# Three units in the first quarters, one SP ring for loads and transposes, layer norm of chunk 1 ahead of the first gates

## The chip, the core and the metric

The kernel runs on one core of a Trainium2 chip. The metric is device time in microseconds (us) of one execution; lower is better. Before the change the median of three runs is 571.9 us (571.53 to 572.21). The core has TensorE (PE in the profile, with its weight loads as PEld), VectorE (DVE), ScalarE (ACT), GpSimd (POOL) and SyncE (SP). Each takes its instructions in program order. SP, ACT and POOL also issue DMAs, each on a queue of its own, and 16 DMA engines move the data.

## What is computed

```python
x  = A_x                                   # 2048 x 448, bf16
xn = layernorm(x)
# A: sliding block of a cache: the last 512 of 2048 keys, 16 query heads of 256, 8 kv heads
q  = xn @ wq                               # 448 -> 4096
p  = softmax(q k^T / 16)                   # 2048 x 512 for each head
s  = concat(p v) @ wo                      # 4096 -> 448
# B: gated feed-forward of 1792 columns
g  = silu((gelu(xn @ w_gate) * (xn @ w_up)) @ w_down)
return x + s * g
```

## The kernel before

The 2048 rows are 16 tiles of 128 (`t`), four tiles make a chunk of 512 (`c`). All engines' instructions are recorded in one list; a small planner (`Plan`) derives the waits from readers and writers of each buffer and then emits each engine's instructions in the order in which they were recorded. So the order of the calls is the order on every engine and on every queue.

First comes the feed-forward part. A **unit** (`n`, 56 in all) is one block of 128 of the 1792 columns for one chunk: gate and up, each 448 deep. 448 is three times 128 and a rest of 64, and everything is cut into halves of 64 rows, so that a matmul on rows 0 to 63 and one on rows 64 to 127 run side by side. `group` writes a unit in two phases, of eight matmuls (with the rest rows, `wgur`) and of six; a unit takes two neighbouring PSUM banks, of the eight. Units go in groups of two; a group is 28 matmuls of 512 columns. `gu_evac` empties a unit: gelu on ACT from the gate's bank into `gl`, then a multiply on DVE of the up's bank and `gl` into `actT`. After a chunk's 14 units, `down` multiplies `actT` by `wd` (56 matmuls), and ACT and DVE make of it `g2`, which is the silu gate doubled.

Layer norm goes by tile: statistics on DVE (`ln_stats`), the inverse deviation either with ACT and DVE (tiles 0 to 3) or on POOL (`ln_rstd_pool`, the others), the normalized tile `xn` on DVE (`ln_norm`), and a transpose to `xnT`. Tiles 0 to 3 are transposed by PE (`ln_tp_pe`, into PSUM, with a copy by ACT or DVE), the others by a DMA transpose on SP (`ln_tp_dma`).

The **head** is the start: the first two units are computed in four quarters (`part`), of 128 columns each, as soon as each of tiles 0 to 3 is there. After each later unit's evacuation, `ln_step` does one step of the layer norm of the next tile: statistics, then, a unit later, norm and transpose.

Loads: x tiles 0 to 3 and the first weights on SP and ACT, further weights and x tiles 4 to 7 on SP, all at the start. Weights come in three blocks of columns whose bounds are in `FBL`. POOL loads x tiles 8 to 11, `wd` and x tiles 12 to 15 after units 4, 6 and 8; when the last tile is normalized, `wq`, V, `wo` and the first tiles of x for the residual (`xr`) on POOL, and K, with a DMA transpose, on SP.

Then comes attention: for each chunk, and each half of eight heads (`g`), four `q_group` of two heads make `qT`; for each head `s_mm` makes the scores and ACT their exponentials (`expT`), `pv` multiplies by V, DVE divides (`onorm`), and DMA transposes on SP make `oT`. `wo_mm` and `wo_fin` multiply by `wo`, gate, add x and store. The last chunk's `down` stands behind the first scores. In SBUF the attention tiles lie over the feed-forward ones; `K.reuse` adds the waits for that.

Of the kernel before, what the change touches and what calls it, by code (L numbers as in the profile page):

```python
# [5 lines left out]
ACT = mybir.ActivationFunctionType  # L6
# [5 lines left out]
P = 128  # L12
# [152 lines left out]
def bass_recurrent_scan__sliding_block_cached__geglu_ffn__prompt_kernel(  # L165
# [18 lines left out]
    NT = S // P  # L184
# [17 lines left out]
    with es:  # L202
# [50 lines left out]
        NXR = 4  # L253
# [21 lines left out]
        FBL = [0, 2, 6, NF]  # L275
# [6 lines left out]
        NGL = 4  # L282
        gl, a, at = place("gl", [P, NGL, QC], BF16, at=at)
        b_gl = sbuf_bufs(a, QC * 2, NGL)
        qT, a, at = place("qT", [P, HG, 2, QC], BF16, at=rf)
        b_qT = [[K.buf(a + (h * 2 + e) * QC * 2, QC * 2) for e in range(2)] for h in range(HG)]
        NEX = 3
        expT, a, at = place("expT", [P, NEX, NJ, QC], BF16, at=at)
# [4 lines left out]
        oT, a, at = place("oT", [P, NCO, QC], BF16, at=at)  # L293
        b_oT = [[K.buf(a, at - a) for t in range(4)] for p in range(Hq // 2)]

# [5 lines left out]
        out_view = out.rearrange("b (t p) d -> p (b t) d", p=P)  # L301

# [39 lines left out]
        load_wr("sp", 0, 1)  # L342
# [16 lines left out]
        load_w("sp", 2, 1)  # L359

# [57 lines left out]
        def group(units, x, lo, hi, start, stop, reads):  # L418

            for ph in range(2):
                for i, (b, w, wr) in enumerate(units):
                    lst = []
                    for k in ([NK] if ph == 0 else []) + list(range(NK)):
                        for u, j in ((0, ph), (1, 1 - ph)):
                            rows = slice(R * u, R * u + R)
                            l = wr[rows] if k == NK else w(j, k)[rows]
                            lst.append((bank[b + j][:, lo:hi], l, x(k)[rows], start and k == NK,  # L430
                                        stop and ph == 1 and k == NK - 1))
                    o = mms(lst, reads, b_ps[b:b + 2], [last_row[b]] if b in last_row else [])
                    last_row[b] = o

        def xs(c, lo=0, hi=QC):
            return lambda k: xnT[:, k, c * QC + lo:c * QC + hi]

        def gu_group(n, b, part=None):

            c, f0 = divmod(n, NF)  # L440
            units, deps = [], [b_wgu]
            for i in range(2):
                f = f0 + i
                wi = [j for j in range(3) if FBL[j] <= f][-1]
                deps += b_wl[wi] + b_wlr[min(wi, 1)]
                cols = slice(f * P, (f + 1) * P)
                units.append((b + 2 * i, lambda j, k, cols=cols: wgu[:, j, k, cols], wgur[:, cols]))
            lo, hi = (0, QC) if part is None else (part * P, (part + 1) * P)
            group(units, xs(c, lo, hi), lo, hi, lo == 0, hi == QC,
                  deps + b_xnT[c * 4 + lo // P:c * 4 + hi // P])  # L450
# [8 lines left out]
        def down(c, b0):  # L459
            for t4 in range(4):  # L460
                t = c * 4 + t4
                b = b0 + t4
                mms([(bank[b][:, 0:D], actT[:, c % 2, f, t4 * P:(t4 + 1) * P], wd[:, f, :], f == 0, f == NF - 1)
                     for f in range(NF)], [b_wd] + b_actT[c % 2], (b_ps[b],))
                s = t % 2
                act(tmp[:, s, :], bank[b][:, 0:D], ACT.Tanh, (b_ps[b],), b_tmp[s], scale=0.5)
                K.op("dve", lambda e, t=t, b=b, s=s: e.scalar_tensor_tensor(  # L467
                    out=g2[:, t, :], in0=tmp[:, s, :], scalar=1.0, in1=bank[b][:, 0:D],
                    op0=ALU.add, op1=ALU.mult), b_tmp[s] + [b_ps[b]], (b_g2[t],))

        def ln_first(t):
            ln_stats(t)
            ln_std_act(t)
# [10 lines left out]
        ln_tp_pe(0, 4, "act")  # L484
        ln_stats(2)
        ln_std_act(2)
        ln_tp_pe(1, 5, "dve")
        gu_group(0, 0, 0)
        gu_group(0, 0, 1)
        ln_second(2)  # L490
        ln_first(3)
        ln_tp_pe(2, 6, "act")
        gu_group(0, 0, 2)
        ln_second(3)
        ln_tp_pe(3, 7, "dve")

        act(tmp[:, 1, 0:1], nhalf[:, :], ACT.Gelu_apprx_tanh, (b_nhalf,), (b_tmp[1][0],))
        gu_group(0, 0, 3)
# [15 lines left out]
        DOWN_AT = {NF + 2: 0, 2 * NF + 2: 1, 3 * NF + 2: 2}  # L514
        cur = 0
        ln_t = [4, 4]

        def ln_step():

            t = ln_t[0]  # L520
            if t < NT and t == ln_t[1]:
                ln_stats(t)
                ln_rstd_pool(t)
                ln_t[0] += 1
            elif ln_t[1] < NT:
                t = ln_t[1]
                ln_norm(t)
                ln_tp_dma(t)
                ln_t[1] += 1

        for n in range(0, NQC * NF, 2):
            if n > 0:
                gu_group(n, cur)
            gu_evac(n, cur)
            if n > 0:
                ln_step()
            gu_evac(n + 1, cur + 2)
            if n > 0:
                ln_step()
            cur = 4 - cur  # L540
            if n == 4:
                load_x("pool", 8, 4)
            if n == 6:
                dma("pool", wd[:, :, :], B_w_down.rearrange("(f p) d -> p f d", p=P), (), (b_wd,))
            if n == 8:
                load_x("pool", 12, 4)
            if ln_t[1] == NT:
                ln_t[1] += 1
                for g in range(NG):
                    load_wq(g)  # L550
                for g in range(Hkv):
                    load_v(g)
                for g in range(Hkv):
                    load_k(g)
                K.reuse(b_wo)
                for i in range(NCO // 8):
                    dma("pool", wo[:, i * 8:(i + 1) * 8, :],
                        A_wo.rearrange("(c p) d -> p c d", p=P)[:, i * 8:(i + 1) * 8, :], (), (b_wo[i],))
                for t in range(NXR):
                    dma("pool", xr[:, t, :], x_view[:, t, :], (), (b_xr[t],))  # L560
            if n + 2 in DOWN_AT:
                down(DOWN_AT[n + 2], cur)
                cur = 4 - cur

        act(tmp[:, 1, 0:1], nhalf[:, :], ACT.Exp, (b_nhalf,), (b_tmp[1][0],))


        def q_group(c, h, b):

            units = [(b + 2 * i, lambda j, k, i=i: wq[:, k, (h + i) * Dh + j * P:(h + i) * Dh + (j + 1) * P],  # L570
                      wqr[:, h + i, :]) for i in range(2)]
            group(units, xs(c), 0, QC, True, True, b_wql[h // HG] + b_xnT[c * 4:c * 4 + 4])
            for i in range(2):
                h8, bb = h % HG + i, b + 2 * i
                act(qT[:, h8, 0, :], bank[bb], ACT.Copy, (b_ps[bb],), (b_qT[h8][0],))
                K.op("dve", lambda v, h8=h8, bb=bb: v.tensor_copy(qT[:, h8, 1, :], bank[bb + 1]),  # L576
                     (b_ps[bb + 1],), (b_qT[h8][1],))

        def s_mm(h, b0):
            h8, g = h % HG, h // 2  # L580
            x = h % NEX
            for jp in range(NJ // 2):
                for j in (2 * jp, 2 * jp + 1):
                    mms([(bank[b0 + j], kT[:, g, e, j * P:(j + 1) * P], qT[:, h8, e, :], e == 0, e == 1)
                         for e in range(2)], [b_kT[g]] + b_qT[h8], (b_ps[b0 + j],))
                pb = b0 // 2 + jp
                act(expT[:, x, 2 * jp:2 * jp + 2, :], pall[pb][:, :].rearrange("p (j q) -> p j q", j=2), ACT.Exp,
                    (b_ps[2 * pb], b_ps[2 * pb + 1]), (b_exp[x][jp],), scale=att_scale)

        def pv(h, b0):  # L590
# [3 lines left out]
            for t4 in range(4):  # L594
                bb = b0 + t4
# [38 lines left out]
        K.reuse([b for y in b_qT for b in y])  # L634
        bx, by = cur, 4 - cur
        for c in range(NQC):
            for g in range(NG):
                h0 = g * HG
                for i in range(0, HG, 2):
                    q_group(c, h0 + i, (bx, by)[i // 2 % 2])  # L640
                if c == 0 and g == 0:
                    K.reuse([b for x in b_exp for b in x])
                s_mm(h0, bx)
                if c == 0 and g == 0:
                    down(NQC - 1, by)
                    K.reuse([b for x in b_on for b in x])
                    K.reuse([b for x in b_oT for b in x])
                elif g == 0:
                    for t4 in range(4):
                        wo_mm(t4, by + t4, 0, NCO)  # L650
                        wo_fin(c - 1, t4, by + t4)
# [7 lines left out]
        wo_mm(0, bx, 0, LATE)  # L659
        wo_mm(1, bx + 1, 0, LATE)  # L660
        wo_mm(0, bx, LATE, NCO)
        wo_fin(c, 0, bx)
        wo_mm(1, bx + 1, LATE, NCO)
        wo_fin(c, 1, bx + 1)
        wo_mm(2, bx + 2, 0, NCO)
        wo_fin(c, 2, bx + 2)
        for i in range(2):
            b = (bx + 3, by)[i]
# [57 lines left out]
```

## Time and profile before

| | us |
|---|---|
| median of three runs | 571.9 |
| the profiled execution | 571.32 |
| its span, first to last instruction | 569.3 |
| PE, matmul from `xnT` and weights of the feed-forward (744 and 124 of them) | 84.5 and 23.0 |
| PE, `down` | 43.1 |
| PE, Q | 93.3 |
| x tiles 4 to 7, one load on SP, from issue to landing | 7.5 |
| x tiles 8 to 11 and 12 to 15 on POOL, issue to landing | 4.5 and 8.7 |
| `wd` on POOL, issue to landing | 9.3 |
| DMA transposes into `xnT`, 12, issue to landing (least, median, most) | 2.4, 3.0, 12.8 |

All durations and instants come from the one profiled execution; an instant is counted from the start of the span. Half-row matmuls run in pairs, so the busy times of PE's groups overlap in part and don't add up. A row of the list of waits says: engine and tile that waited, what it waited for, total, number of times, longest. In a row of the timeline stand start, length, engine, line, operation, output and inputs, shapes, count; in brackets the idle time before it and what ended it. In the list of windows each engine has its busy time and number of instructions, and the row ends with the clock that was granted to TensorE (1.00 is full), the mean busy share of the DMA engines and the GB/s that they moved.

### The profile page before, as it was taken

The page shows a single profiled execution, that of the slowest core. Times are in us where ns is not written, and L with a number is a line of the kernel's source. Part 1 is how long each engine was busy: PE and PEld are TensorE (multiplying, and loading weights), DVE is VectorE, ACT ScalarE, POOL GpSimd, SP SyncE. Part 2 cuts the span into 40 slices and gives each one's busy share as a digit, 9 for nine tenths or more (in the row PEclk, how much of TensorE's full clock was granted, in tenths as well). Part 3 has the DMA queues.
Part 4 walks back from the last instruction along what each step waited for, and adds up shares of the span by engine and source line. Part 5 has one row for each costly group of instructions (what it writes and reads, how often), then busy time and mean ns, then how long its engine had stood idle before and what let it go on. Part 6 is the DMA issues. An engine that isn't in the chain of part 4 may idle for free.

```text
span 569.3 us, 9817 instructions
## 1 busy us (share of the span) xinstructions
PE 555.1 (98%) x4068; PEld 312.0 (55%) x4104; DVE 279.6 (49%) x756; ACT 210.7 (37%) x276; POOL 35.5 (6%) x67
## 2 busy tenths in 40 slices
PE   8959999999999999999999999999999999999998
PEld 5524444444466466455655654566466455656656
DVE  5733834334256557413664661167367224665632
ACT  4312323335345364402535532054553303536500
POOL 0410382000000000000000000000000000000000
PEclk9979999999999999999999999999999999999999
DMA  8470199920014224211440540124124011341421
GB/s 242 127 159 9 38 271 275 266 45 1 1 27 75 47 34 79 38 31 35 67 84 0 77 73 17 32 54 84 29 48 90 13 33 43 74 66 28 75 47 32
DMA packets 94859, 40.84 MB, mean 72 GB/s; under 512 B 85968, under 2 KB 90624, under 8 KB 94816
## 3 DMA queue, kind: packets, MB, share of 16 engines
q1 hardware_dynamic: 90192, 26.01, 24.2%
q0 software_dynamic: 3936, 13.80, 8.2%
q8 instruction: 32, 0.52, 0.4%
q10 hardware_dynamic: 688, 0.43, 0.3%
q14 instruction: 11, 0.09, 0.1%
HBM read 17.92 MB, written 1.84 MB: 35 GB/s over the span
## 4 chain that ended last, share of the span: by engine, by line
PE 93%; DVE 3%; DMA 2%; issue 1%; POOL 1%; ACT 0%; DVEq 0%
PE bank L317 93%; DMA xnT<-xn 1%; DVE stats L363 1%; DVE xn L382 1%; DVE actT L456 1%; DMA x_67<-in_A_x_dram 0%; POOL rstd L369 0%; DVE mv L364 0%; POOL ve L367 0%; DVE xnT L405 0%; DVE g_58 L467 0%; ACT xnT L311 0%; ACT gl L311 0%; ACT tmp L311 0%; DVE tmp L625 0%
## 5 line engine op out<-in xcount | busy, mean ns | idle before, releaser
L311 ACT ACTIVATE expT<-bank 128x1024 bf16<-128x1024 f32 x128 | 123.8, 1022 | 150.6 <-PE bank L317 150.5
L602 DVE TENSOR_SCALAR onorm<-bank,rden 128x256 bf16<-128x256 f32 x256 | 123.9, 484 | 9.1
L317 PE MATMUL bank<-va,expT 128*128 128x257 bf16 x1024 | 124.0, 273 | 0.0
L317 PE MATMUL bank<-qT,kT 128*128 128x512 bf16 x476 | 115.9, 379 | 2.8 <-ACT qT L311 1.3
L317 PEld LDWEIGHTS bank<-va,expT 128*128 128x128 bf16 x1024 | 99.2, 98 | 27.3 <-DVE onorm L602 1.3
L317 PE MATMUL bank<-wo,oT 128*128 128x448 bf16 (+1 forms) x544 | 97.6, 341 | 0.0
L317 PE MATMUL bank<-xnT,wq 64*128 64x512 bf16 x768 | 93.3, 376 | 0.0
L317 PE MATMUL bank<-xnT,wgu 64*128 64x512 bf16 (+1 forms) x744 | 84.5, 361 | 0.0
L317 PEld LDWEIGHTS bank<-qT,kT 128*128 128x128 bf16 x512 | 49.1, 97 | 52.2 <-issue 3.4
L317 PEld LDWEIGHTS bank<-wo,oT 128*128 128x128 bf16 x544 | 53.1, 98 | 44.0
L600 DVE RECIPROCAL rden<-bank 128x1 f32<-128x1 f32 x256 | 41.0, 160 | 67.2 <-PE bank L317 67.2
L311 ACT ACTIVATE qT<-bank 128x512 bf16<-128x512 f32 x64 | 38.2, 597 | 79.8 <-PE bank L317 78.2
L576 DVE CAST qT<-bank 128x512 bf16<-128x512 f32 x64 | 42.9, 692 | 47.1 <-PE bank L317 47.1
L317 PEld LDWEIGHTS bank<-xnT,wq 64*128 64x128 bf16 x768 | 37.4, 94 | 44.7
L317 PEld LDWEIGHTS bank<-xnT,wgu 64*128 64x128 bf16 x744 | 36.5, 95 | 37.9 <-issue 2.0
L456 DVE TENSOR_TENSOR actT<-bank,gl 128x512 bf16<-128x512 f32 x56 | 37.3, 685 | 37.3 <-ACT gl L311 23.4
L311 ACT ACTIVATE gl<-bank 128x512 bf16<-128x512 f32 x56 | 33.2, 597 | 58.8 <-PE bank L317 58.2
L625 DVE SCALAR_TENSOR_TENSOR tmp<-bank,g_58 128x448 f32<-128x448 f32 (+1 forms) x17 | 10.2, 597 | 82.5 <-PE bank L317 82.5
L317 PE MATMUL bank<-wd,actT 128*128 128x448 bf16 x224 | 43.1, 353 | 0.0
L317 PEld LDWEIGHTS bank<-wd,actT 128*128 128x128 bf16 x224 | 21.7, 98 | 21.2 <-issue 1.3
L305 POOL DMA_DIRECT2D xr<-in_A_x_dram x16 | 8.6, 540 | 382.8 <-DVE ofin L628 382.8
L317 PE MATMUL bank<-xnT,wgur 64*128 64x512 bf16 (+1 forms) x124 | 23.0, 364 | 7.1 <-DMA xnT<-xn 5.8
(38 smaller groups left out, 135.6 us busy)
## 6 DMA issues: line engine op xcount, KB each, us to landing
wo<-in_A_wo_dram POOLq DMA_DIRECT2D x4, 896.0 KB, 19.7
wq<-in_A_wq_dram POOLq DMA_DIRECT2D x2, 1536.0 KB, 10.0
va<-in_A_v_cache_dram POOLq DMA_DIRECT2D x8, 256.0 KB, 13.6
oT<-onorm SPq DMA_TRANSPOSE x128, 2.5
xr<-in_A_x_dram POOLq DMA_DIRECT2D x16, 112.0 KB, 2.3
out_dram<-ofin SPq DMA_DIRECT2D x15, 112.0 KB, 1.7
wd<-in_B_w_down_dram POOLq DMA_DIRECT2D x1, 1568.0 KB, 9.3
x_67<-in_A_x_dram POOLq DMA_DIRECT2D x2, 448.0 KB, 6.6
```

The costliest lines, as they stand in the source:

```text
L305: K.op(q, lambda e, o=o, i=i: e.dma_start(o, i), reads, writes, dma=True)
L311: K.op("act", lambda e, o=o, i=i: e.activation(o, i, func, scale=scale), reads, writes)
L317: ins = e.matmul(o, lhsT=l, rhs=r, start=st, stop=sp)
L363: K.op("dve", lambda e: e.bn_stats(stats[:, t, :], x4[:, t, :]), (b_x4[t],), (b_stats[t],))
L382: K.op("dve", lambda e, lo=lo, hi=hi, src=src: e.tensor_scalar(xn[:, s, lo:hi], x4[:, t, src:src + hi - lo], mv[:, t, 0:1], rstd[:, t:t + ...
L456: K.op("dve", lambda e: e.tensor_tensor(actT[:, c % 2, f, :], bank[b + 1], gl[:, s, :], ALU.mult), (b_ps[b + 1], b_gl[s]), (b_actT[c % 2][ ...
L576: K.op("dve", lambda v, h8=h8, bb=bb: v.tensor_copy(qT[:, h8, 1, :], bank[bb + 1]), (b_ps[bb + 1],), (b_qT[h8][1],))
L600: K.op("dve", lambda e, bb=bb, r=r: e.reciprocal(rden[:, r:r + 1], bank[bb][:, Dh:Dh + 1]), (b_ps[bb],), (b_rden[r],))
L602: K.op("dve", lambda e, bb=bb, r=r, t4=t4: e.tensor_scalar(onorm[:, o, t4, h % 2, :], bank[bb][:, 0:Dh], rden[:, r:r + 1], None, op0=ALU.m ...
L625: K.op("dve", lambda e: e.scalar_tensor_tensor(out=tmp[:, s, c0:c1], in0=bank[b][:, c0:c1], scalar=0.5, in1=g2[:, t, c0:c1], op0=ALU.mult, ...
```

## The change

- The head takes three units (`HEAD`, banks 0 to 5), not two; the PE transposes use banks 6 and 7, those of tiles 0, 1 and 3 are copied by ACT, that of tile 2 by DVE, and tiles 2 and 3 are transposed together after the second quarter. The groups of two units are then (3, 4), (5, 6) and so on up to (53, 54); bank pairs are named one by one, since the units of a group no longer lie in four neighbouring banks (`bk` finds the bank of an index).
- The weight blocks begin at 0, 3 and 8 instead of 0, 2 and 6.
- x tiles 8 to 15 are loaded on SP, issued at the start behind the last weights. `wd` is loaded on SP, issued behind the transpose of tile 8. The rest rows of the first up weights go from SP to ACT's queue.
- `ln_step` becomes `ln_a` (statistics, inverse deviation) and `ln_b` (norm and transpose). Statistics of tiles 4 and 5 and the norm and transpose of tile 4 stand ahead of the evacuation of the first three units. Then each group has one `ln_b` between its two evacuations and one `ln_a` after them.
- The loads for attention are recorded at unit 31. `down(2)` moves from the feed-forward loop to the first scores, ahead of `down(3)`.
- The last unit (55) is alone: its first phase, the first Q group, then its second phase and evacuation, then three more Q groups.
- Memory: three slots instead of four for `gl` and `xr`; `expT` and `onorm` lie over the gate weights, `oT` over `wd` and `actT`, and `qT` from `gl` on, its heads in reverse order (`qs`).

```diff
-        NXR = 4
+        NXR = 3
...
-        FBL = [0, 2, 6, NF]
+        FBL = [0, 3, 8, NF]
...
-        NGL = 4
+        NGL = 3
...
+        def qs(h):
+            return HG - 1 - h % HG
...
-        load_wr("sp", 0, 1)
+        load_wr("act", 0, 1)
...
         load_x("sp", 4, 4)
         load_w("sp", 2, 0)
         load_w("sp", 2, 1)
+        load_x("sp", 8, 4)
+        load_x("sp", 12, 4)
...
+        def bk(pairs, j):
+            return pairs[j // 2] + j % 2
...
-        ln_tp_pe(0, 4, "act")
+        ln_tp_pe(0, 6, "act")
         ln_stats(2)
         ln_std_act(2)
-        ln_tp_pe(1, 5, "dve")
-        gu_group(0, 0, 0)
-        gu_group(0, 0, 1)
+        ln_tp_pe(1, 7, "act")
+        ln_first(3)
+        HEAD, PH = (0, 1, 2), (0, 2, 4)
+        gu_group(HEAD, PH, 0)
+        gu_group(HEAD, PH, 1)
         ln_second(2)
-        ln_first(3)
-        ln_tp_pe(2, 6, "act")
-        gu_group(0, 0, 2)
         ln_second(3)
-        ln_tp_pe(3, 7, "dve")
+        ln_tp_pe(2, 6, "dve")
+        ln_tp_pe(3, 7, "act")
 
         act(tmp[:, 1, 0:1], nhalf[:, :], ACT.Gelu_apprx_tanh, (b_nhalf,), (b_tmp[1][0],))
-        gu_group(0, 0, 3)
+        gu_group(HEAD, PH, 2)
+        gu_group(HEAD, PH, 3)
...
-        DOWN_AT = {NF + 2: 0, 2 * NF + 2: 1, 3 * NF + 2: 2}
+        DOWN_AT = {NF + 2: 0, 2 * NF + 2: 1}
...
+        ln_a()
+        ln_a()
+        ln_b()
+        gu_evac(0, 0)
+        gu_evac(1, 2)
+        gu_evac(2, 4)
+        NU = NQC * NF
+        cur, nxt = (6, 0), (2, 4)
+        for n in range(3, NU - 1, 2):
+            gu_group((n, n + 1), cur)
+            gu_evac(n, cur[0])
+            ln_b()
+            gu_evac(n + 1, cur[1])
+            ln_a()
+            cur, nxt = nxt, cur
+            if n == 9:
+                dma("sp", wd[:, :, :], B_w_down.rearrange("(f p) d -> p f d", p=P), (), (b_wd,))
+            if n == 31:
...
+                    u = NU - 1
+                    gu_group((u,), cur[:1], phases=(0,))
+                    q_group(c, h0, (cur[1], nxt[0]))
+                    gu_group((u,), cur[:1], phases=(1,))
+                    gu_evac(u, cur[0])
...
                 s_mm(h0, bx)
                 if c == 0 and g == 0:
+                    down(NQC - 2, by)
                     down(NQC - 1, by)
```

## The prediction

> **What bounds the kernel now.** I read the page's shares first, then the slices, then the list of waits, then the stage that these point to.
>
> ```profile
> span 569.3 us, 9817 instructions
> PE 555.1 (98%) x4068; PEld 312.0 (55%) x4104; DVE 279.6 (49%) x756; ACT 210.7 (37%) x276; POOL 35.5 (6%) x67
> PE   8959999999999999999999999999999999999998
> PEclk9979999999999999999999999999999999999999
> DMA  8470199920014224211440540124124011341421
> PE bank L317 <- DMA xnT<-xn: 5.8, 1, 5.8
> ```
>
> TensorE is busy 98% of the span, so only its gaps and slow stretches can be won. The one hole is the third of 40 slices (28.5 to 42.7 us): PE 5 tenths, clock 7. The list of waits names it: one wait of 5.8 us for a DMA transpose into `xnT`; no other wait of PE adds up to more than 1.3 us. The windows and the timeline of that stage (start, length, engine, what):
>
> ```profile
> 28.00:32.00 4.00, 3.24 (x30) 1.47 (x26) 3.48 (x9) 2.03 (x4) 1.32 (x3) 1.00 1.01 328
> 32.00:36.00 4.00, 0.00 (x0) 0.00 (x0) 2.00 (x6) 0.00 (x0) 0.79 (x2) 0.78 1.24 203
> 36.00:40.00 4.00, 2.92 (x14) 1.22 (x16) 0.00 (x0) 0.00 (x0) 0.00 (x0) 0.50 0.40 70
> 40.00:44.00 4.00, 4.00 (x26) 1.85 (x23) 1.58 (x4) 1.18 (x2) 0.09 (x1) 0.87 0.01 4
> ...
> 37.08 0.61 PE L317 MATMUL bank<-xnT,wgur 64*128 64x512 bf16 x2 [5.85 <-DMA xnT<-xn]
> 42.17 6.04 PE L317 MATMUL bank<-wd,actT 128*128 128x448 bf16 x31
> ```
>
> In a window's row the second number is PE's busy time; the last three are granted clock, DMA share and GB/s. PE stops at 31.24, starts at 37.08 (5.84 us), and runs its next group at half clock: 37.08 to 42.17 is 5.09 us for 28 matmuls that take 3.02 elsewhere (groups start at 55.69, 58.71, 61.73). The hole costs 5.84 + 2.07 = **7.91 us**.
>
> Its cause is DMA. A transpose issued at 19.37, with idle DMA engines, landed in 2.5 us; those of tiles 6 and 7, at 25.9 and 28.5, took 10.9 and 8.5. Between them the POOL queue had put `wd` (1568 KB, issued 24.64, 9.3 us) and x tiles 12 to 15 (27.68) on the same engines, whose share was 1.0 or near it from 28 us on.
>
> **The change, part by part.** Most edits move work whose PE time stays: 56 units, 4 `down`, all Q groups.
>
> *Loads and transposes in one ring.* `wd` and x 8 to 15 leave POOL for SP: x behind the weights, `wd` behind tile 8's transpose. [...] The rows say that what counts is what is in flight at the time (2.5 against 10.9), and that does change. Tile 7's transpose follows the evacuation of the third group after the head. With my head and first wait (below), that group ends at 25.3; its multiply and norm (0.68 and 0.61 us) bring the issue to 26.6, landing at 29.1 to 29.6 by the rows of 2.5 to 3.0. The first unit of chunk 1 is now second in the sixth group, at 31.3 + 0.86 = 32.2. Some 2.6 us are to spare, and `wd` is not issued before 30.9. I take the row: **7.91 us go**.
>
> *Three units in the head.* Before: first gates at 7.13, head done at 12.90, two units. A part of two units takes 0.97 us (7.13 to 8.10), so three take 1.44. The first gates need 1120 KB (x 448, weights 672) where 896 KB landed by 7.07; 224 KB at the 277 to 305 GB/s of that stretch are 0.8 us, less 0.5 since a 0.59 us issue leaves SP for ACT while the engines stood at 0.60 share (3 to 4 us): start 7.35. Two parts to 10.23; four plus four transposes, 0.80; the first copy on DVE (0.42) ends 0.05 after them; two parts more: 14.0. The old head and one more unit (1.51) would have ended at 14.41: **gain 0.4**, between 0.9 and -0.4 as weights land at 7.1 or at 8.0. The second copy goes from DVE to ACT, ending near 8.2, before the second part's turn at 8.8. The extra issue on ACT (0.5 us) delays the table load to 2.6 + 1.28 + 0.20 = 4.1, ahead of the first square root at 4.39.
>
> *Layer norm ahead of the first gates.* This adds a wait. DVE is taken in order, and the statistics of tiles 4 and 5 and the norm of tile 4 now stand before the multiplies that free the banks of units 0 to 2. They wait for x tiles 4 to 7 (one load). It landed at 13.24 before, unnoticed, since its first reader ran at 16.83:
>
> ```profile
> 16.83 0.62 DVE L363 BATCH_NORM_STATS2 stats<-x_67 128x6 f32<-128x448 bf16 x1
> 17.75 0.22 POOL L367 TENSOR_SCALAR ve<-mv 128x1 f32<-128x1 f32 x1 [16.29 <-DVE mv L364]
> 18.73 0.61 DVE L382 TENSOR_SCALAR xn<-x_67,mv,rstd 128x448 bf16<-128x448 bf16 x2 [0.48 <-POOL rstd L369]
> 19.25 0.68 DVE L456 TENSOR_TENSOR actT<-bank,gl 128x512 bf16<-128x512 f32 x1
> ```
>
> From the first of these to the end of the multiply are 3.10 us. With x landing at X, unit 0's banks are free at X + 3.15. PE needs them for unit 4, after unit 3's first phase (four pairs of 0.216): 14.0 + 0.86 = 14.86. Stall: X - 11.7. Ahead of x stand 384 KB more (224 in the first weights, 160 in the second block). At 250 to 300 GB/s that is 1.3 to 1.6 us, less for longer rows (768 and 1280 B, were 512 and 1024) and the issue saved: I take 0.65, X = 13.9, **cost 2.2**. Bounds: X = 13.0 costs 1.3; X = 14.8 costs 3.1; with the wait gone the gelu and multiply still end at 15.0, 0.15 late. The gate is the second price. [...] The row: PE idle from 31.24, clock 1.00 to 34, 0.63 in 34 to 35 (with 0.50 after, a drop at 34.26), so 3.0 after. [...] I go by the row for the far end.
>
> *`wd` late.* The first down comes at 37.4 (seven groups after the head, plus the stall). Tile 8's transpose is issued at 29.65 and takes 1.2; `wd` follows at 30.85. Its only row, 9.3 us, had company: it would give 2.75 of stall. A lone 112 KB load took 2.8, and 1456 KB more at 345 GB/s (28 to 31 us) 4.3: 7.2 with rounding, landing at 38.05, **cost 0.65**; at 390 GB/s (13 us) it is 6.6, costing 0.1.
>
> *Nothing.* Gates in steady state: DVE carries the same two multiplies, norm and statistics (2.75 of each 3.02 us). The last unit around the first Q: between gates and Q (134.71) PE has no gap now; each bank pair still has 1.7 us or more for a 1.4 us evacuation; table load hidden behind a Q group as before. `down(2)` moved next to `down(3)`: same 56 matmuls, DVE and ACT idle beside them. `xr` with three slots: reload 2.3 us, next use a tile's 6 us `wo` chain away or more. `wq` and `va` loads start some 11 us earlier on POOL, needed after 134. If a junction's cover were gone, it would cost one evacuation, 1.4.
>
> Sum: -7.91 - 0.41 + 2.2 + 0.65 = **-5.5**. The span becomes 563.8, the profiled execution (571.32, 2.02 outside its span) 565.8; the median of runs, 571.9, lies 0.58 higher: **566.4**.
>
> **Rivals.**
> - *Likeliest, 0.57*: the sum; with its terms, 565 to 568.
> - *The new waits are covered, 0.18*: x by 12, `wd` by 37.4; -7.91 - 0.41 + 0.15, so **563.7**. For: DMA reached 374 to 393 GB/s on long rows (12 to 15 us). Against: x would have to land earlier than before with 384 KB more ahead.
> - *One late load closes the gate, 0.15*: X = 14.8, 3.1 of wait and 2.07 at half clock; 566.4 + 0.9 + 2.07 = **569.4**. For: 231 to 257 GB/s at 8 to 12 us, engines full.
> - *The single ring is slow, 0.07, slower*: the same low rate at both places. From x after 14.8 and `wd` over 9.7 us each wait closes the gate, and the costs pass 8.3. At x 15.5 and `wd` 10.4: 2 x (3.8 + 2.07) = 11.7 - 8.3 = +3.4, **575.3**. Against: both would have to run below their contended rows.
> - *Not as said, 0.03*: tile 7 lands late all the same, its 2.6 us used up, the hole half left: about **572**.
>
> Range: 563.3 to 569.8 takes in the first three. Within 0.2% (1.1 us, about what this kernel's measurement can tell from none) 0.02; slower 0.08; faster 0.90.
>
> **What would show it.** PE's wait for `xnT` transposes gone, and clock 1.00 at 32 to 42 us; transposes of tiles 4 to 7 under 3 us. First part near 7.35, the 512-column gates near 14.0, x 4 to 7 landing near 13.9. A wait of PE of about 2 us for DVE `actT` near 15 to 17, then one under 1 us for `wd` near 37. I am wrong if the first exceeds 3 us and the clock falls, if PE waits for `xnT` near 32, or if a gap appears at the first Q.

## The result and the profile after

The changed kernel takes 566.27 us (median of four, 565.96 to 568.52), the kernel before 571.77 in the same comparison; the ratio is 0.9911, 95% interval 0.9885 to 0.9938. It is faster by 5.5 us. The profiled execution took 565.96 us, its span 564.1.

The page of the changed kernel, the lines that answer to those shown of before:

```profile
span 564.1 us, 9925 instructions
PE 552.3 (98%) x4110; PEld 310.7 (55%) x4146; DVE 279.0 (49%) x755; ACT 211.1 (37%) x277; POOL 32.7 (6%) x64
PE   7899999999999999999999999999999999999997
PEclk9999999999999999999999999999999999999999
DMA  8560599900024124011430430134033012421431
```

The third slice of PE has gone from 5 to 9 and its clock from 7 to 9. The list of waits, PE alone, first 60 us:

```profile
PE bank L322 <- DVE actT L461: 1.8, 1, 1.8
PE bank L322 <- ACT ve L380: 1.3, 1, 1.3
PE bank L322 <- DMA wd<-in_B_w_down_dram: 1.3, 1, 1.3
```

The wait for `xnT`, 5.8 us, is gone, and the transposes show why. Tile 6's, with the us from issue to landing, before (issued from 25 to 26 us, with `wd` under way) and after (22 to 24 us):

```profile
wd<-in_B_w_down_dram POOLq DMA_DIRECT2D x1, 1568.0 KB, 9.3
xnT<-xn SPq DMA_TRANSPOSE x1, 10.9
```

```profile
xnT<-xn SPq DMA_TRANSPOSE x1, 2.4
```

Tile 7's, for which PE had stood still, went from 8.5 to 2.4 us. Two new waits stand here (DVE `actT`, `wd`), and one at 8.27 us that the list puts down to ACT `ve`. That ACT instruction had ended at 8.17, but the first gates read nothing of it; the last of their weights landed at about the same time (the rest rows, issued at 2.12 on SP, took 5.8 us; those on ACT's queue 5.9), so I take it as a wait for weights; the lists of other runs name it so (`wgur`). The same stretch in the windows and the timeline:

```profile
32.00:36.00 4.00, 4.00 (x40) 1.84 (x38) 3.50 (x10) 1.19 (x2) 0.79 (x2) 1.00 0.90 282
36.00:40.00 4.00, 2.74 (x22) 1.19 (x17) 3.46 (x9) 1.19 (x2) 0.79 (x2) 1.00 0.86 188
...
8.27 0.23 PE L322 MATMUL bank<-xnT,wgur 64*128 64x128 bf16 x2 [1.28 <-ACT ve L380]
...
16.87 0.39 PE L322 MATMUL bank<-xnT,wgur 64*128 64x512 bf16 x2 [1.84 <-DVE actT L461]
...
38.59 10.75 PE L322 MATMUL bank<-wd,actT 128*128 128x448 bf16 x56 [1.26 <-DMA wd<-in_B_w_down_dram]
```

PE is busy and at full clock where it had stood still (from 36 to 40 us, 2.74 us busy, but for the wait for `wd`). Before, the first `down` began at 42.17 with 16 units done; now it begins at 38.59 with 17. A unit is 1.51 us, so 42.17 + 1.51 - 38.59 = 5.1 us are won up to there, of 5.2 in the span.

### The profile page after: what moved, and what is told of

Read it like the earlier page. It is cut to its first block, busy times and chain, and to the rows that moved or that the text cites. A ratio compares the mean times of both kernels' runs of the same rounds, so it can differ in the third digit from the quotient of the medians.

```text
span 564.1 us, 9925 instructions
## 1 busy us (share of the span) xinstructions
PE 552.3 (98%) x4110; PEld 310.7 (55%) x4146; DVE 279.0 (49%) x755; ACT 211.1 (37%) x277; POOL 32.7 (6%) x64
## 3 DMA queue, kind: packets, MB, share of 16 engines
HBM read 17.92 MB, written 1.84 MB: 35 GB/s over the span
## 4 chain that ended last, share of the span: by engine, by line
PE 94%; DMA 3%; DVE 1%; SPq 1%; issue 1%; ACT 0%; POOL 0%; DVEq 0%
PE bank L322 94%; DMA x_67<-in_A_x_dram 1%; DMA wd<-in_B_w_down_dram 1%; SPq L310 1%; DVE actT L461 0%; DVE stats L370 0%; DVE xn L389 0%; DVE g_58 L472 0%; ACT gl L316 0%; POOL rstd L376 0%; ACT tmp L316 0%; DVE tmp L629 0%; DVE ofin L632 0%; POOL ve L374 0%; DVE mv L371 0%
## 5 line engine op out<-in xcount | busy, mean ns | idle before, releaser
L322 PE MATMUL bank<-xnT,wgu 64*128 64x512 bf16 (+1 forms) x780 | 82.4, 346 | 0.0
L322 PEld LDWEIGHTS bank<-xnT,wgu 64*128 64x128 bf16 x780 | 35.6, 94 | 37.2
L472 DVE SCALAR_TENSOR_TENSOR g_58<-tmp,bank 128x448 bf16<-128x448 f32 x16 | 9.9, 621 | 34.9 <-ACT tmp L316 34.9
```

The source lines that it names most:

```text
L322: ins = e.matmul(o, lhsT=l, rhs=r, start=st, stop=sp)
```

## Experiments

All times are medians, against the kernel before on the same chip (571.9 to 572.3). My theory after the result: the hole went since nothing heavy is in flight beside the transposes of tiles 5 to 7; what is left are two waits, DVE's line for x and the late `wd`, which can be taken away one by one. Rivals: the queue itself (POOL against SP) made the hole; or the head and the early layer norm are needed for it; or the two waits are not independent.

### What filled the hole: the queue, or the moment

E3 and E4 issue `wd` at one place in the record, behind tile 6, on either queue.

```diff
-            if n == 9:
+            if n == 5:
                 dma("sp", wd[:, :, :], ...)     # E3
+                dma("pool", wd[:, :, :], ...)   # E4, in its place
```

> The changed kernel with wd issued on SP behind the transpose of tile 6, so that the transpose of tile 7 is behind wd in the same queue. If a queue is served in order: wd issued near 24.8, landed near 32.4, tile 7 landed after it, near 33.5 to 34.5, and a wait for xnT of 1.5 to 2.5 us at 32.0; the wait for wd is gone; time 566 to 567.5. If DMAs of one queue overlap freely: tile 7 lands within 4 us of its issue, near 30.5, no wait, time 565.

> The same place in the recorded order, but wd on POOL's queue, as in the kernel before; issued near 25.8, behind POOL's work for tile 7's deviation. My theory (what is in flight counts, not the queue): tile 7's transpose, issued near 26.6 beside it, takes 6 to 9 us as in the kernel before (8.5 and 10.9) and lands at 33 to 36; a wait for xnT of 1 to 3.5 us at 32.0, time 566 to 569. Rival (queues are served by turns, so that a small transpose in another queue gets through): it lands within 4 us, near 30.5, no wait, time 565. If SP's order alone gives the wait and POOL's does not, the one ring is a burden and not the gain.

Measured: 566.93 and 568.45 us, two executions each, so the reading rests on the records. PE's timeline, of E3 and then of E4, at the first group with chunk 1:

```profile
34.01 0.39 PE L322 MATMUL bank<-xnT,wgur 64*128 64x512 bf16 x2 [1.61 <-DVE actT L461]
```

```profile
35.11 0.39 PE L322 MATMUL bank<-xnT,wgur 64*128 64x512 bf16 x2 [2.61 <-DVE mv L371]
```

The releasers named are the last marks of DVE, but this is the first unit of chunk 1, which reads `xnT`, and tile 7's transpose landed 0.1 us earlier (33.91 and 35.02). It was issued at 26.8 on SP's queue behind `wd` (25.03, landed 8.3 us later, at 33.3) and took 7.1 us; with `wd` on POOL's (26.13, 8.5 us) it was issued at 27.5 and took 7.6. In the changed kernel, with no bulk ahead of it, it takes 2.4. So in both records the transpose landed after the bulk load that was issued ahead of it, in the same queue or in another. The rival falls: neither queue let it through. What removed the hole is the order in time.

E5 puts that part alone on the kernel before: x tiles 8 to 15 at the start on SP, `wd` on SP behind tile 7's transpose; head and layer norm untouched.

```diff
         load_w("sp", 2, 1)
+        load_x("sp", 8, 4)
+        load_x("sp", 12, 4)
...
-            if n == 4:
-                load_x("pool", 8, 4)
-            if n == 6:
-                dma("pool", wd[:, :, :], ...)
             if n == 8:
-                load_x("pool", 12, 4)
+                dma("sp", wd[:, :, :], ...)
```

> The kernel before with the queue part of the change alone: x tiles 8 to 15 on SP at the start, wd on SP behind the transpose of tile 7; head, blocks and order of layer norm stay. My theory: transposes of tiles 6 and 7 land 2.4 to 3 us after issue, tile 7 near 31.2, so the wait for xnT at 31.2 falls from 5.84 to 0.5 or less and the half clock there goes, 7.4 to 7.9 us saved. wd, issued near 29.8 and 7.6 us under way, lands at 37.4 where the first down is ready at 34.3: a new wait of 3 us. Net 571.8 - 7.7 + 3.1 = about 567.2, and some 2 more if the clock falls in that wait. Rival (the hole needs the three units and the early layer norm, which place chunk 1 later and its transposes earlier): the wait for xnT stays above 3 us, time 570 or more.

Measured: 567.81 us, ratio 0.9925 (0.9906 to 0.9944). PE's waits of E5, and its timeline at the first `down`:

```profile
PE bank L317 <- DMA wd<-in_B_w_down_dram: 3.2, 1, 3.2
...
37.50 12.44 PE L317 MATMUL bank<-wd,actT 128*128 128x448 bf16 x56 [3.21 <-DMA wd<-in_B_w_down_dram]
```

No wait for `xnT` is left, so the hole needs neither the three units nor the early layer norm. The expected wait for `wd` came, 3.2 us, and the clock fell in it: `down` took 12.44 us, not 10.75. This part alone gives some 4.3 of the 5.5 us. In the changed kernel the first `down` is ready at 37.3 instead of 34.3, since 17 units and not 16 stand ahead of it and PE waits 1.84 us on the way, while `wd` is issued only 1.1 us later. No run has the head or the early layer norm alone.

### The two waits that are left

E2 issues `wd` one group earlier, E6 one later.

```diff
-            if n == 9:
+            if n == 7:    # E2; E6: n == 11
                 dma("sp", wd[:, :, :], ...)
```

> The changed kernel with the load of wd issued one group earlier, behind the transpose of tile 7 and not of tile 8. My theory (the 1.3 us wait before the first down is the load's own 7.6 us from a late issue): issued near 27.8, landed near 35.5, ahead of 37.2; the wait goes, time 566.3 - 1.3 = 565.0. Tile 8's transpose lands later, near 36, and nobody waits. Rival (the load runs into tile 7's transpose, which was issued 1.2 us before it, as in the kernel before): tile 7 lands 3 us or more later than 2.4 us after issue, a wait for xnT at 32 us, and no gain.

> The changed kernel with wd issued one group later, behind the transpose of tile 9: the wait before the first down is made longer by one group, 3.0 us, to about 4.3 us, to see when the clock falls. By what the kernel before showed (clock down 3.0 us after PE's last work, back 3.9 us after its next): the clock is at half for some 5 us, about 4 of them with PE at work, costing 2 us; time 566.3 + 3.0 + 2.0 = 571.3. If a gap of this length does not close the gate: 569.3.

E2: 565.55 us (0.9883, 0.9863 to 0.9903), and no wait for `wd` in its list. `wd` was issued at 27.67 and took 8.9 us, tile 7 landed in 2.4 us; tile 8 took 7.6, and PE did not wait for it. E6: 571.93 us. Its wait, and the clock:

```profile
41.98 13.12 PE L322 MATMUL bank<-wd,actT 128*128 128x448 bf16 x56 [4.42 <-DMA wd<-in_B_w_down_dram]
PEclk8998999999999999999999999999999999999999
```

The wait is 4.42 us, as expected, with half clock from 40.0 to 46.8; `down` took 13.12, 2.4 more than at full clock. Those 2.4 and the 3.2 us of longer wait are the loss. The clock was down in the head too (the first 8), but that cost only some 0.2: the next matmuls wait for DVE's line behind x anyway, here 0.58 us and not 1.84, and start at 17.09 instead of 16.87. One group's delay of one load gives back the whole gain of the change.

E1 puts the layer norm of tiles 4 and 5 behind the first evacuations.

```diff
-        ln_a()
-        ln_a()
-        ln_b()
         gu_evac(0, 0)
         gu_evac(1, 2)
         gu_evac(2, 4)
+        ln_a()
+        ln_a()
+        ln_b()
```

> The changed kernel with the statistics of tiles 4 and 5 and the norm and transpose of tile 4 put behind the evacuation of units 0 to 2. My theory (the wait of 1.84 us for DVE actT at 15.0 is only DVE standing in line for the load of x tiles 4 to 7): the wait falls to 0.2 or less, the first group at full width takes about 3.1 us and not 5.0, and the time falls by 1.7 to 1.9 us, to about 564.4. The wait for wd stays at 1.3 us, since everything behind moves up together. Rival (PE would wait at that place anyway, for banks or for weights of the second block): the wait is renamed and stays above 1 us, time 566. Second rival (layer norm of chunk 1 needs that early start): tile 7's transpose lands after the first unit of chunk 1 wants it, a new wait for xnT near 30 us, no gain or a loss.

Measured: 567.79 us, no gain. PE's waits of E1:

```profile
PE bank L322 <- DVE stats L370: 3.4, 1, 3.4
PE bank L322 <- ACT ve L380: 1.3, 1, 1.3
PE bank L418 <- DVE epst L353: 1.2, 1, 1.2
PE bank L404 <- DVE xn L389: 0.5, 2, 0.3
PE bank L322 <- DVE actT L461: 0.4, 1, 0.4
```

The wait for DVE went from 1.84 to 0.4, nearly as I held (0.2 or less); but 3.4 us stand at the first `down`, where `wd` is late (the releaser named is an old one: `wd`, issued at 32.67, took 7.7 us and landed at 40.4, and `down` began at 40.55). The wait moved. DVE shows why:

```profile
23.56 0.61 DVE L389 TENSOR_SCALAR xn<-x,mv,rstd 128x448 bf16<-128x448 bf16 x2 [0.47 <-POOL rstd L376]
26.58 0.61 DVE L389 TENSOR_SCALAR xn<-x,mv,rstd 128x448 bf16<-128x448 bf16 x2 [0.48 <-POOL rstd L376]
29.64 0.61 DVE L389 TENSOR_SCALAR xn<-x,mv,rstd 128x448 bf16<-128x448 bf16 x2 [0.48 <-POOL rstd L376]
```

One norm each 3.02 us, with a wait of 0.48 for POOL's deviation: two multiplies, norm, statistics and that wait fill a group of PE exactly. The layer norm can't catch up, so tile 8's norm is at 29.64 instead of 28.97, its transpose's issue takes 2.35 us instead of 1.19, and `wd` behind it is at 32.67 instead of 30.83. The second rival was wrong in its place (tile 7 was in time) and right in kind. Besides, this record's head was at half clock for 3.4 us (8.08 to 11.49); the one execution without (mean clock 1.000) has a span of 564.5, against 564.1 to 564.5 of the changed kernel's.

E8 makes both edits.

> The changed kernel with both edits: layer norm behind the first evacuations and wd behind tile 7's transpose. If the two waits are independent: -1.8 and -1.3, about 563.2, with no wait of PE over 0.5 us after 12 us. Rival (the first edit moves PE up by 1.8 us while the ring still carries x tiles 8 to 15 until 19 us, so transposes or wd become late again): a wait of about 1 us for wd or xnT comes back, 564 to 564.5.

Measured: 564.72 us (0.9872, 0.9851 to 0.9892), waits of 0.4 us for DVE and 0.4 for `wd`; `wd` took 9.4 us. Better than either edit, but 1.5 us short of the sum of the two waits. The clock is no reason in its record (562.6 of span), where it is full from 7.15 us on: the first gates start at 8.61, 0.34 us later than in the changed kernel, the two waits of 0.4 are left, and 0.3 go in the matmuls behind the first of them, which take 2.46 us (15.75 to 18.21) instead of 2.17.

E7 puts the last unit whole ahead of the first Q.

```diff
-                    gu_group((u,), cur[:1], phases=(0,))
-                    q_group(c, h0, (cur[1], nxt[0]))
-                    gu_group((u,), cur[:1], phases=(1,))
+                    gu_group((u,), cur[:1])
                     gu_evac(u, cur[0])
+                    q_group(c, h0, (cur[1], nxt[0]))
```

> The changed kernel with the last unit whole, ahead of the first Q group, and not around it. My costing put the interleaving at nothing: time 566.3 within 0.3, and no wait of PE over 0.3 us near 130 to 136 us. Rival (a lone unit's second phase waits for the first phase of the same banks, so that the interleaving saves time): a gap of 0.2 to 0.5 us between its phases and 566.5 to 566.8.

Measured: 567.29 us. The unit takes 1.75 us (120.30 to 122.05); around the Q group its phases take 0.86 and 0.65, 1.51 together. So 0.24 us is what the interleaving spares, and PE shows no other gap there. The rest of the difference isn't at this place: in this record `wd` took 8.8 us, not 7.6, PE waited 2.48 for it and the clock fell, with nothing changed there; `down` took 12.25. Whole-run times of this kernel can't price 0.3 us.

### What scatters: the clock in the head

Executions of one kernel differ by up to 2.7 us, in part with the mean clock: of the changed kernel 564.1, 564.2 and 564.5 us of span at 0.999 to 1.000, 566.6 at 0.997. In E2 and E7 it is not so: the execution at 1.000 (563.6 and 565.3) is not the shortest (562.6 and 565.0, both at 0.997). Only the profiled execution shows where the clock fell. In E1, E2 and E6 it was at half for 3.4 us in the head; in E7, at 0.997 too, it was full there and fell in the wait for `wd`. E9 and E10 fill the gap ahead of the first gates with 11 idle matmuls of 256 columns, in the changed kernel and in E8.

```diff
         ln_first(3)
+        warm(11, 5)
         HEAD, PH = (0, 1, 2), (0, 2, 4)
```

> The changed kernel with 11 more idle matmuls (128x256, about 0.11 us each, on a bank that is overwritten later) between the transposes of tiles 0 and 1 and the first gates. In the records of three of the runs so far the clock is at half for 3.2 to 3.5 us in the head, after a gap of 1.3 to 1.6 us ahead of the first gates, which costs 1.6 us. Theory (the gap that the later weights leave lets the clock gate close, in some executions and not in others): with the gap filled no execution has a mean clock of 0.997 or less, the times lie within 0.7 us of each other, and the median is 565.8 to 566.3, against 568.5 in the worst of the changed kernel's. Rival (the scatter comes from the DMAs or from the record's own state): executions with 0.997 go on, about every second one.

> The same 11 matmuls in the kernel with layer norm behind the first evacuations and wd behind tile 7's transpose. If the filled gap keeps the clock: median 562.8 to 563.5, as the undisturbed executions of that kernel had (561.1 and 562.6 of span), and none above 564. Rival: median at 564.7 as without.

Measured: 567.33 and 566.50 us (E8: 564.72), with 0.997 in three executions of six and three of five: no gain, as the rival has it. In the changed kernel there was little to gain in the head: with half clock there, the matmuls that wait for x still started at 16.70 in E2 and at 17.09 in E6, against 16.87. Both records have full clock in the head, and a new gap, of 2.13 and 2.21 us, with no releaser. E10's, and from its DMAs of 14 to 16 us the row of a queue of instructions (packets, MB, share):

```profile
16.91 0.71 PE L322 MATMUL bank<-xnT,wgu 64*128 64x512 bf16 x3 [2.21 <-issue]
...
q8 instruction: 1, 0.02, 3.5%
```

The gap stands between two matmuls of one recorded operation, so no semaphore is behind it. In E10 the clock fell 0.4 us after its end, in E9 it did not. The packet, of 16 KB, began at 14.47 us (E9: 14.62), with all DMA engines busy (a mean share of 1.0 or more), and took 1.1. PE stopped at 14.70 (14.83), in both records after 449 of its matmuls and weight loads, and went on 1.3 (1.2) us after the packet had landed. E8's record has such a packet up to 15.56 and a short stop after the same count, until 16.90. In E12 the packet landed at 15.29, and PE came to that count only at 16.75. So the gap fits a wait for instructions that come late; no run tests that by itself.

Both E11 and E12 are on E8's kernel. In E12 the gap of the head is filled with fewer instructions: the start's idle matmuls become 10 of 512 columns in place of 20 of 256, and 6 more follow; E11 has only the first of the two, as a control.

```diff
-                    ins = e.matmul(bank[b][:, 0:256], lhsT=gl[:, 0, 0:P], rhs=gl[:, 0, 0:256], ...)
+                    ins = e.matmul(bank[b][:, 0:512], lhsT=gl[:, 0, 0:P], rhs=gl[:, 0, 0:512], ...)
...
-        warm(20, 3)
+        warm(10, 3)
...
+        warm(6, 5)        # E12 only
```

> The kernel with layer norm behind the first evacuations and wd behind tile 7's transpose, its first idle matmuls written as 10 of 512 columns in place of 20 of 256: the same time at the start with 10 fewer matmuls in PE's instruction stream, and no filling of the gap ahead of the first gates. Control for the next run. Expected: as without the edit, 563.2 to 565.4 with a median near 564.7, executions of mean clock 0.997 or less among them.

> The same with 6 more idle matmuls of 512 columns in the gap ahead of the first gates: the gap filled, and 4 matmuls fewer in PE's stream than without either edit. The 11 short ones of the last pair of runs left the clock of the head alone in both records, but a gap of 2.1 us without a releaser stood inside unit 3's first phase. If that gap comes from the place in the instruction stream, it is gone here, and with the head's clock kept the median is 563.0 to 563.5 and no execution is above 564.2. If scatter of 1.5 us or more remains, its cause is not, or not only, the gap ahead of the first gates.

E11: 565.04 us, three of four at 0.997. E12: **564.06 us** (563.65 to 564.24; ratio 0.9857, 0.9843 to 0.9872), all four at 1.000. PE's timeline of the head, E11 and then E12 (the second quarter pair follows the transposes of tiles 2 and 3):

```profile
8.28 0.29 PE L322 MATMUL bank<-xnT,wgur 64*128 64x128 bf16 x2 [1.56 <-DMA wgur<-in_B_w_up_dram]
12.28 0.62 PE L404 MATMUL bank<-ident,xn 128*128 128x128 bf16 x8
```

```profile
6.30 1.46 PE L418 MATMUL bank<-gl 128*128 128x512 bf16 x6
8.52 0.23 PE L322 MATMUL bank<-xnT,wgur 64*128 64x128 bf16 x2 [0.76 <-DMA wgur<-in_B_w_up_dram]
10.97 0.62 PE L404 MATMUL bank<-ident,xn 128*128 128x128 bf16 x8
```

Two quarters take 4.00 us in E11 and 2.45 in E12, with a gap of 1.56 and 0.76 ahead of them; the clock was at half from 8.15 to 11.56 us in E11 and full in E12. So with the gap filled all four executions have a mean clock of 1.000, where three of E11's four have 0.997; the fall cost 1.55 us in this record, in a kernel in which no wait for x hides it. E12 is the fastest version, 2.2 us below the changed kernel's median; E11's one execution at 1.000, 563.81 us, is as fast.

The first `down` shows after which waits the clock fell (that fall is the prediction's gate). PE's timeline there, in E1 and in E7:

```profile
40.55 10.75 PE L322 MATMUL bank<-wd,actT 128*128 128x448 bf16 x56 [3.45 <-DVE stats L370]
```

```profile
39.89 12.25 PE L322 MATMUL bank<-wd,actT 128*128 128x448 bf16 x56 [2.48 <-DMA wd<-in_B_w_down_dram]
```

After 3.45 us the clock was still full in E1; after 2.48 it had fallen in E7. So in these two the length of the wait did not decide. In every record in which the clock changed, its changes lie 3.41 us or a whole multiple of it apart: it was at half from 39.53 to 42.95 in E7, from 38.08 to 41.49 in E5, from 34.25 to 41.08 before (6.83, two steps). I divided each record into such steps, counted from its changes, and added up PE's idle time in each step up to the first `down`:

| | PE idle in one step at full clock, us |
|---|---|
| the clock fell at the step's end | head: E6 1.82, E1 1.86, E2 2.01, E11 2.11; later: E7 2.12, E10 2.21, E6 2.42, E5 2.84, before 3.01 |
| it held, the longest | changed kernel 1.84, E4 1.77, E1 1.75 and 1.70, E3 1.67 |

My estimate from these rows, for these fourteen records, is a limit near 1.8 of 3.41 us. E1's 3.45 us fell into two steps, 1.70 and 1.75, and the clock held; 2.12 of E7's 2.48 fell into one. The steps lie elsewhere in each record: in the head the clock fell at 7.96 us in E2, at 8.08 in E1, at 8.15 in E11 and at 9.26 in E6. That fits what the gap ahead of the first gates did: the clock fell with 1.34 us of it in E1, 1.55 in E2, 1.56 in E11 and 1.64 in E6, and held with 1.62 in E3, 1.76 in E8 and 1.77 in E4.

## Why the prediction was right

It said 566.4 (563.3 to 569.8); measured 566.27. The mechanism is the one it named; that the number agrees to 0.13 us is luck. Counted from start to start in the two records, the hole gave 8.1 us and the head 0.4, and the two waits cost 2.0 and 1.4: 5.1 up to the first `down`, where it said 5.5, while the changed kernel's executions lie 2.6 us apart. By its steps:

- **The hole, -7.91.** Right. No wait for `xnT`, clock 1.00 from 32 to 42 us, transposes of tiles 5 to 7 in 2.4 us; tile 4's took 5.7, behind x tiles 8 to 15, where under 3 was said. E3, E4 and E5 show the reason that the row gave, what is in flight. The issuing engine decided little: `wd` ahead of tile 7 made its transpose 7.1 us on SP's queue and 7.6 on POOL's, against 2.4 in the changed kernel. That `wd` leaves the queue is not the gain; that it leaves that moment is.
- **The head, -0.4.** Right in sum by luck, from two errors that cancel. The first gates began at 8.27, not 7.35: I gave 0.5 us back for SP's saved issue, and the weights came 0.9 later than that. But a quarter of three units takes 1.17 us, not 1.44 (8.27 to 9.44): I scaled the 0.97 of two units, in which the 14 pairs come 69 ns apart, while 21 pairs come at 56. The 512-column gates began at 14.00, as said.
- **DVE's line for x, +2.2.** Right: x landed at 13.77 (said 13.9) and its first reader started at once; the banks were free 3.1 us later. The wait is 1.84 us, the group 2.0 late.
- **`wd`, +0.65.** Mis-sized: the load took 7.6 us, not 7.2, and the stall is 1.26 (1.4 against the place at which `down` would have begun, 37.2). In other runs it took up to 9.4. My estimate took a rate from the best stretch, and added it to a "lone" load of 2.8 us that was one of four issued within 0.5 us.
- **Nothing.** Held: no wait at the first Q; E7 prices what the interleaving spares at 0.24.
- **The gate.** Wrong as a threshold, without harm to the sum. From one row I took 3.0 us of idleness as the point at which the clock falls. In these records the falls go with how much of one step of 3.41 us PE stood still (a fall after 1.82 us and more, none after 1.84 and less), by my estimate with a limit near 1.8. With the wait for x, 1.84 us in one step, the clock just held; 2.2 us in one step, as predicted, would by this estimate have lowered it, so that the price was nothing is luck. This scatter was in none of my rivals.
- **Rivals.** Covered waits (563.7) was not reached: both waits were there. It took four more edits to get to 564.06: layer norm behind the evacuations, `wd` a group earlier, fewer and longer idle matmuls at the start, and the filled gap.

## What to carry to other kernels

When a small transfer on the critical path is slow, look at what bulk was issued before it, in any queue, and move that in time: here the transpose took 7.1 us behind `wd` on SP's queue, 7.6 behind `wd` on POOL's and 2.4 with no bulk ahead of it. An in-order engine whose cycle just fits the group of the bound engine has no room to catch up: in E1, with 3.02 us of DVE for each group, tile 8's norm stayed 0.67 us later, and `wd`, recorded behind it, was issued 1.84 later. A short gap of PE in a start-up phase is worth filling, with few instructions, where no later wait hides what it costs (1.55 us in E11). Look at PE's idle time per step of the clock, not at one wait's length: in these records, with steps of 3.41 us, the clock held over a wait of 3.45 us in E1 and fell in one of 2.48 in E7.

## What was not expected of the hardware

- In the records in which it changed, the granted clock did so only at steps of 3.41 us, at another instant in each (half from 39.53 to 42.95 us in E7, from 38.08 to 41.49 in E5). It fell after steps in which PE stood still for 1.82 us (E6) or more and held after those with 1.84 (changed kernel) or less; a wait of 3.45 us in E1, split into 1.70 and 1.75, left it full.
- In the head it fell with gaps of 1.34 us (E1), 1.55 (E2), 1.56 (E11) and 1.64 (E6), and not with 1.62 (E3), 1.76 (E8) and 1.77 (E4), and stayed at half for 3.4 us. That cost 1.55 us in E11, and 0.2 or nothing in E6 and E2, where PE waits for x behind it.
- A gap of 2.13 (E9) and 2.21 us (E10) without a releaser appeared inside one group of matmuls when 11 matmuls were added ahead of it, with a 16 KB packet of instructions under way (E10: 14.47 us, for 1.1), and not when the filling took fewer instructions (E12).
- `wd`, the same 1568 KB, took 7.6 (changed kernel) to 9.4 us (E8) from issue to landing on SP's queue.
